# Seven block products in place of eight for 18 couples of an expert layer

## The chip, the core and the metric

The kernel runs on one core of a Trainium2 chip. Five engines work side by side, each on its own list of instructions in order: TensorE (PE) multiplies matrices out of SBUF into PSUM, VectorE (DVE) and ScalarE (ACT) work elementwise and can read PSUM, GpSimd (POOL) works elementwise in SBUF and issues the indirect transfers, SyncE (SP) issues all other transfers. PSUM has 128 partitions in eight banks; one bank holds 128 x 512 numbers of 32 bits. The metric is the time of one execution in microseconds; before the change the median of three runs is 1423.42 us (1422.26 to 1426.2).

## The reference

```python
X = np.fft.rfft(x, axis=1)                       # x: 8 batches of 2496 x 256
Yr = Xr @ w_r - Xi @ w_i + b_r                   # complex mixing, 256 x 256
Yi = Xr @ w_i + Xi @ w_r + b_i
Y  = soft-threshold of Yr and Yi by 0.01
x  = np.fft.irfft(Y, n=2496, axis=1)             # now 19968 tokens of 256
logits = x @ w_gate                              # 8 experts
e_idx  = argmax(logits); gate_w = softmax(logits)[e_idx]
eom    = 1 / (1 + exp(-(x @ w_output_gate)))
for e in range(8):
    h  = np.maximum(x[mask] @ w1[e], 0.0)        # w1[e]: 256 x 1024, the up-product
    ye = h @ w2[e]                               # w2[e]: 1024 x 256, the down-product
    out[mask] = gate_w * eom[:, e] * ye
```

The output is 19968 x 256 in 32-bit floats. The kernel represents a 32-bit number as a high and a low half in 16-bit floats and makes each product of three: high by high, high by low, low by high.

## The kernel before

The first part goes through the eight batches: a Fourier transform in two stages of matmuls (lines 715 and 793), the mixing (823), the inverse in two stages (853 and 919), the gate's logits (964). The tokens with their gate factors are written to a table `yd` in device memory. Meanwhile the expert weights are read, scaled by a power of two for each expert, split into halves (lines 1118 to 1123, on ACT, POOL and DVE) and stored as `wd`, 2 MB for each expert.

Routing runs twice, on DVE above all: `routing(0)` after four batches, `routing(1)` after eight. Each gives tiles of 128 tokens of one expert, with indices to gather their rows and to scatter their results. The 160 tiles are 71 couples of two tiles that share an expert (`PAIRS`, tiles 0 to 141), and 18 mixed tiles of two half tiles of different experts. The first 32 couples (tiles 0 to 63) are of the first phase; couples 32 to 70 are the second phase, with the mixed tiles strewn among them (`BLOCKS`).

For a tile, `gathers` issues the indirect read on POOL; `tokens` finds a scale on DVE (lines 438 to 449), the factor (1507), the high half on ACT (1512) and the low half on DVE (1513), and SP issues a transposing transfer into `eT` (1526). For a couple, `block` starts four pieces of `up`, each filling a PSUM bank with 12 matmuls of 256 token columns (1617): two blocks of 128 hidden units, each 2 halves of the contraction by 3 half products. ACT applies the ReLU and writes the high half of the hidden values (1627), DVE the low half (1628). `down` multiplies by the second weights, one bank a tile with 24 matmuls of 256 columns (1581), ACT scales the result (1597), POOL scatters it (1600).

Weights of couples lie in three buffers `wbuf`, used in turn (`wplace`; the couples of one buffer go through the experts in order, so that most transfers are found unneeded on the chip and skipped). `fetch` and `half_fetch` issue the conditional transfers on SP, the up-half and the down-half of 1 MB each (1461), after the product that last used that half. The mixed tiles have two buffers of their own, laid over the first part's `bt` and `bdt`.

The order of all this isn't found on the chip: `Issue` is a planner that plays the program through while it is built. Each piece of work is a Python generator that yields the engine it needs, a priority (a due time, smaller first) and an assumed duration; when an engine is free in the plan, the waiting piece with the smallest due time is issued. `Slots` and `Places` hold back a piece until a buffer is free, and a bank has to be free for each product. The resulting order of each engine is fixed; on the chip an engine waits for the next instruction of its list. The constants at the head of the file (`P`, `UP`, `DN`, `AHEAD`, `RT`, `WF` and so on) are due times and the depth of lookahead.

```python
i, pt = yield "P", r, 1.42 if len(w) > 1 else (1.34, 1.31)[m - 1], f, True
yield "A", r, 0.6, lambda: A.activation(hv[:, 0], pt, AF.Relu)
yield "D", r, 0.69, lambda: V.scalar_tensor_tensor(hv[:, 1], pt, 0.0, hv[:, 0], ALU.max, ALU.subtract)
```

Of the kernel before, what the change touches and what calls it, by code (L numbers as in the profile page):

```python
# [27 lines left out]
NQ = 22  # L28
P3 = 3 * N1
# [107 lines left out]
P = 69.07  # L137
TP, TE, QT = -14.75, -31.33, 31.33
# [3 lines left out]
S2 = 28.15  # L142
E1 = 55.66
DS = 3.39
ES = 7.69
Z1 = 39.76
Z2 = 21.97
IV = -7.74
IS = 2.63
GO = -33.61  # L150
R0 = 25.15
R1, G1 = 6.43, 0.54
GA = 0.66
W0 = 10.67
W1 = 30.32
TG = 54.25
# [5 lines left out]
XL, TA, TB, YS, WL, WS = -82.07, -9.26, -27.11, 68.34, 21.07, 89.6  # L162
# [3 lines left out]
UP, DN = 1.32, 10.12  # L166
AHEAD = 6
# [3 lines left out]
LR = 9.25  # L171
QN, QY, QV, QX, QZ, QU = -11.85, 13.43, 208.83, 73.36, 34.2, 102.95
RA, QE = -58.63, -33.84
SA = 35.74
SE = 78.16
Z3 = 16.69
BE = 49.35
YE = 51.81
PB = -2.78, -1.54, 0.72, 8.85, 1.32, 0.97, 8.27, 4.18
XC = 7.0, 0.1, 5.4, 0.1, 3.0, 0.1  # L180
RT = -33.27
WT = 0.0
WF = 24.23
QO = -60.23
# [143 lines left out]
def tile_fft_moe(ctx, tc, x, w_r, w_i, b_r, b_i, w_gate, w_og, w1, w2, f1, f4, cmat, gmat, m16, out, dbg=None):  # L328
# [30 lines left out]
    wd = pd.tile([E, 128, 8192], F16, name="wd")  # L359

# [35 lines left out]
    isc = pc.tile([128, E], F32, name="isc")  # L396
    A.activation(isc, cnt[-1], AF.Exp)
# [83 lines left out]
    whl = pf.tile([128, 2, 2, 512], F16, name="whl")  # L481
# [11 lines left out]
    yt = [py.tile([P3, 4, ROW], F32, name=f"yt{i}") for i in range(YR)]  # L493
# [9 lines left out]
    slots = {k: Slots(n) for k, n in dict(x=XR - 6, s1=S1 + 1, A=AN, xt=3, z=2, zhl=ZR, bt=1, bd=1, yt=YR, ol0=OL[0], wr=WR - 1, wsp=SR, ol1=OL[1], fac=12, dg=1, gL=1).items()}  # L503
    slots.update({k: Places(range(EARLY[k])) for k in EARLY})
    slots.update(eT1=Places([]), hh1=Places([]))
# [583 lines left out]
    def weights(r, step):  # L1089

        yield "s1", 0
        for u in range(2 * E):
# [9 lines left out]
            def f():  # L1102
                s, si = root2(ma, "swe")
                if m == 0:
                    V.tensor_copy(isc[:, e:e + 1], si)
                else:
                    V.tensor_tensor(isc[:, e:e + 1], isc[:, e:e + 1], si, ALU.mult)
# [289 lines left out]
    W = []  # L1397
# [12 lines left out]
    def open_h():  # L1410
# [11 lines left out]
        yield "lbm", B - 1  # L1422
        for pool, tag in ((pf, "bt"), (py, "bdt")):
            W.append(pool.tile([128, 4 * NQ * 128], F16, tag=tag, name="late" + tag)[:, :8192])
        late = pf.tile([128, K1 * 256], F16, tag="gt", name="lategt")
        for i in range(2):
            parts_["hh", "late", i] = late[:, 2048 * i:2048 * i + 2048]
            parts_["eT", "late", i] = late[:, 4096 + 512 * i:4608 + 512 * i].rearrange("p (m v c n) -> p m v c n", m=1, v=2, c=2)
            for k in ("hh", "eT"):
                io.put(slots[k + "1"], ("late", i))  # L1430
        io.set("late")
# [5 lines left out]
    def before(k):  # L1437

        return None if k < 2 or k == KW else k - 2 if k < KW else k - 3

    def fetch(r):

        yield "w open"
        for k, (t, n) in enumerate(PAIRS):
# [3 lines left out]
            for m in range(2):  # L1448
# [3 lines left out]
                io.at(io.now + (TAIL if before(k) is None else WT), io.set, "w", t, m, 0)  # L1452

    def half_fetch(key, m, c, place, new, r):
# [8 lines left out]
        yield from move(r, 1.05e6 if new else 0, (1.3, 0.4)[m], f)  # L1463
# [226 lines left out]
```

## Time and profile before

| | us |
|---|---|
| median of three runs | 1423.42 |
| the profiled execution | 1422.78 |
| its span | 1421.0 |
| PE busy | 1390.6 (98%) |
| DVE busy | 986.2 (69%) |
| ACT busy | 738.9 (52%) |
| POOL busy | 650.5 (46%) |
| up-products of couples, line 1617, 3408 matmuls of 256 columns | 389.2 |
| down-products of couples, line 1581, 3408 matmuls of 256 columns | 391.0 |

A row of the groups gives line, engine, operation, output and inputs by their names, the tile's shape, the count, the busy time, the mean of one in ns, and then the idle time of the engine ahead of them. The mean of a matmul holds its way through the array, which overlaps with the next ones; the distance between matmuls is read from the starts in the timeline. PEld are the weight loads, which overlap with the matmuls. A row of the stretches gives busy time and count for each engine, the granted clock of PE as a share of full speed, the share of the transfer engines and GB/s. A row of the waits gives total, times and longest. The timeline has start, duration and instruction; idle time ahead of it stands in brackets.

### The profile page before, as it was taken

The page shows a single profiled execution, that of the slowest core. Times are in us where ns is not written, and L with a number is a line of the kernel's source. Part 1 is how long each engine was busy: PE and PEld are TensorE (multiplying, and loading weights), DVE is VectorE, ACT ScalarE, POOL GpSimd, SP SyncE. Part 2 cuts the span into 40 slices and gives each one's busy share as a digit, 9 for nine tenths or more (in the row PEclk, how much of TensorE's full clock was granted, in tenths as well). Part 3 has the DMA queues.
Part 4 walks back from the last instruction along what each step waited for, and adds up shares of the span by engine and source line. Part 5 has one row for each costly group of instructions (what it writes and reads, how often), then busy time and mean ns, then how long its engine had stood idle before and what let it go on. Part 6 is the DMA issues. An engine that isn't in the chain of part 4 may idle for free.

```text
span 1421.0 us, 40860 instructions
## 1 busy us (share of the span) xinstructions
PE 1390.6 (98%) x15696; PEld 1237.5 (87%) x15696; DVE 986.2 (69%) x2849; ACT 738.9 (52%) x1401; POOL 650.5 (46%) x733
## 2 busy tenths in 40 slices
PE   7999999999999999899999999999999999999996
PEld 5998989898988888789998888999989999999996
DVE  5888877789999888668998774555455545554541
ACT  4877687778677765343333344434444434434431
POOL 3464645564567663334455634343343334333311
PEclk9999999999999999999999999999999999999999
DMA  8699989898988898786353373554644565555440
GB/s 212 166 212 230 205 226 207 214 212 224 217 203 188 201 227 190 196 253 174 97 158 78 88 178 80 135 142 128 164 107 103 135 168 132 135 137 139 126 106 23
DMA packets 285997, 231.54 MB, mean 163 GB/s; under 512 B 239246, under 2 KB 248080, under 8 KB 279167
## 3 DMA queue, kind: packets, MB, share of 16 engines
q1 hardware_dynamic: 270377, 187.02, 54.1%
q0 software_dynamic: 15424, 41.90, 12.7%
q8 instruction: 123, 2.02, 0.6%
q14 instruction: 73, 0.60, 0.1%
HBM read 286.72 MB, written 58.52 MB: 243 GB/s over the span
## 4 chain that ended last, share of the span: by engine, by line
PE 83%; DVE 6%; issue 5%; DMA 2%; POOL 2%; ACT 1%; SPq 1%; POOLq 0%; DVEq 0%; ACTq 0%
PE ps L1617 27%; PE ps L1581 26%; PE ps L823 11%; PE ps L715 5%; PE ps L793 3%; PE ps L919 3%; PE ps L853 3%; DMA x<-in_x 1%; PE ps L964 1%; PE ps L758 1%; POOL out L1600 1%; PE ps L817 1%; PE ps L599 1%; PE ps L1385 1%; DVE z L839 1%
## 5 line engine op out<-in xcount | busy, mean ns | idle before, releaser
L1617 PE MATMUL ps<-eT,wbuf 128*128 128x256 f16 x3408 | 389.2, 273 | 3.6 <-DMA wbuf<-wd 3.6
L1581 PE MATMUL ps<-wbuf,hh 128*128 128x256 f16 x3408 | 391.0, 273 | 0.0
L1617 PEld LDWEIGHTS <-wbuf 128*128 128x128 f16 x3408 | 331.6, 98 | 43.7 <-DMA wbuf<-wd 3.8
L1581 PEld LDWEIGHTS <-hh 128*128 128x128 f16 x3408 | 329.0, 98 | 41.9 <-issue 3.8
L1628 DVE SCALAR_TENSOR_TENSOR hh<-ps,hh 128x512 f16<-128x512 f32 x284 | 196.0, 690 | 225.7 <-ACT hh L1627 224.6
L1600 POOL DMA_INDIRECT out<-o,sidx x160 | 166.0, 1038 | 372.7 <-ACT o L1597 351.6
L1627 ACT ACTIVATE hh<-ps 128x512 f16<-128x512 f32 x284 | 169.5, 597 | 231.7 <-PE ps L1617 229.8
L823 PE MATMUL ps<-whl,xt 128*128 128x256 f16 x1920 | 222.6, 273 | 0.0
L1485 POOL DMA_INDIRECT yg<-yd,gidx x160 | 158.2, 989 | 138.7 <-DVE yhl L1513 82.9
L823 PEld LDWEIGHTS <-xt 128*128 128x128 f16 x1920 | 187.8, 98 | 30.9 <-issue 0.6
L1597 ACT ACTIVATE o<-ps,facs 128x256 f32<-128x256 f32 x160 | 75.7, 473 | 178.5 <-PE ps L1581 169.3
L1512 ACT ACTIVATE yhl<-yg,ys 128x256 f16<-128x256 f32 x160 | 80.8, 506 | 66.9 <-DVE ysi L449 31.7
L715 PE MATMUL ps<-f1t,x 117*128 117x120 f32 (+1 forms) x704 | 90.3, 282 | 9.2 <-DMA x<-in_x 7.8
L715 PEld LDWEIGHTS ps<-f1t,x 117*128 117x128 f32 (+1 forms) x704 | 85.6, 197 | 12.6 <-issue 9.1
L843 POOL TENSOR_TENSOR zhl<-z,zhl 128x512 f16<-128x512 f32 x64 | 75.6, 1182 | 30.8 <-ACT zhl L841 15.4
L1513 DVE SCALAR_TENSOR_TENSOR yhl<-yg,ys,yhl 128x256 f16<-128x256 f32 x160 | 78.9, 509 | 14.1 <-ACT yhl L1512 13.9
L842 POOL CAST zhl<-z 128x512 f16<-128x512 f32 x54 | 34.1, 631 | 107.7 <-DVE z L839 76.6
L838 ACT ACTIVATE zhl<-ps,sc 128x512 f32<-128x512 f32 x80 | 54.8, 686 | 39.1 <-PE ps L823 32.1
L1122 POOL TENSOR_TENSOR wsp<-wr,wsp 128x512 f16<-128x512 f32 x58 | 70.7, 1219 | 4.8
L1628 DVE SCALAR_TENSOR_TENSOR lategt<-ps,lategt 128x512 f16<-128x512 f32 x36 | 24.8, 688 | 65.8 <-ACT lategt L1627 65.8
L839 DVE SCALAR_TENSOR_TENSOR z<-ps,zhl 128x512 f32<-128x512 f32 x80 | 54.6, 684 | 20.7 <-ACT zhl L838 19.4
L919 PE MATMUL ps<-bdt,f4t 120*117 120x512 f16 x264 | 68.8, 379 | 0.0
(236 smaller groups left out, 2113.6 us busy)
## 6 DMA issues: line engine op xcount, KB each, us to landing
wbuf<-wd SPq DMA_DIRECT2D x142, 1024.0 KB
latebt<-wd SPq DMA_DIRECT2D x36, 1024.0 KB
latebdt<-wd SPq DMA_DIRECT2D x36, 1024.0 KB
yd<-yt SPq DMA_DIRECT2D x120, 158.4 KB
x<-in_x SPq DMA_DIRECT2D x106, 156.0 KB
wr<-in_moe_w SPq DMA_DIRECT2D x32, 512.0 KB
wd<-wsp SPq DMA_DIRECT2D x64, 256.0 KB
yg<-yd,gidx POOLq DMA_INDIRECT x160
```

The source lines that it names most:

```text
L715: T.matmul(pv[:, dh, :, m * j:m * j + m], xs[:k, j0 + j, 128 * dh:128 * dh + 128], fw, start=True, stop=True)
L823: T.matmul(yp[:, 256 * j:256 * j + 256], xt_[:, v, 2 * dh + j, 64 - 64 * u:192 - 64 * u], whl[:, dh, vw, 256 * u:256 * u + 256], start=Fal ...
L919: T.matmul(pt[:P3], w, src[:, :, :, vb_], start=(n == 0), stop=(n == 2))
L1485: yield "G", r + 5.6 * POS[t] - 30, 1.0, lambda: G.indirect_dma_start(out=yg, out_offset=None, in_=src, in_offset=bass.IndirectOffsetOnAxi ...
L1512: yield "A", r - 10, 0.5, lambda: A.activation(yhl[:, 0], yg[:, :256], AF.Copy, scale=s)
L1513: yield "D", r - 10, 0.48, lambda: V.scalar_tensor_tensor(yhl[:, 1], yg[:, :256], s, yhl[:, 0], ALU.mult, ALU.subtract)
L1581: T.matmul(st["pt", t][1][c * q:c * q + c, :256], hh[:, v, fc, 128 * n + c * q:128 * n + c * q + c], wq[:, fc // 2, vw, fc % 2], start=(fc ...
L1597: yield "A", r - DN, 0.47, lambda: A.activation(o, pt[:, :256], AF.Copy, scale=fac)
L1600: yield "G", r - DN, 1.0, lambda: G.indirect_dma_start(out=outs[POS[t] % 8], out_offset=bass.IndirectOffsetOnAxis(ap=sidx[:, t:t + 1], axi ...
L1617: T.matmul(pt[:, 128 * m * j:128 * m * (j + 1)][:, 64 * q:128 * m - 64 * (len(w) - 1 - q)], wq[:, dh, g // 4, vw, 128 * (g % 4):128 * (g % ...
L1627: yield "A", r, 0.6, lambda: A.activation(hv[:, 0], pt, AF.Relu)
L1628: yield "D", r, 0.69, lambda: V.scalar_tensor_tensor(hv[:, 1], pt, 0.0, hv[:, 0], ALU.max, ALU.subtract)
```

## The change

For 18 couples of the second phase (tiles from 88 on whose weights are in the first or the second of the three buffers: `seven`) the up-product is made otherwise. Tokens are two blocks of 128 (the two tiles), the contraction two blocks of 128, the hidden units two blocks of 512. The product of two 2 x 2 block matrices takes eight block products; Winograd's form of Strassen's method takes seven, with sums of blocks ahead and behind.

- Sums of weights: four for each expert (S1 to S4 of 256 x 1024 as blocks of 128 x 512). `sums` reads `w1` anew, adds on POOL or DVE, scales and splits on ACT and POOL or DVE, and stores them as `wsd`, 1 MB for each expert. It waits until `routing(1)` is at its end. `sum_fetch` brings them next to the weights, two conditional transfers for each of the couples.
- Sums of tokens: `presum` makes four for each couple on POOL, with ACT for the high half.
- `up7` makes the seven products, each one bank of 4 x 3 matmuls of 128 columns. Their sums: the first bank is copied by ACT, the second added by DVE, the third and fourth copied by ACT and added to on POOL, and four banks are completed by DVE in PSUM, with ReLU on ACT and the low half on DVE as before. Only one couple is within its seven products at a time.
- The low half of odd tiles of these couples is made on POOL in place of DVE.
- `AHEAD` goes from 6 to 10 tiles, the assumed time of a weight transfer from 1.05e6 to 1.4e6 over `RATE`, two assumed durations in `tokens` rise, and nearly all due times have new values, those of the first part too.

```diff
-P = 69.07
+P = 68.59
-UP, DN = 1.32, 10.12
-AHEAD = 6
+UP, DN = 3.46, 8.42
+AHEAD = 10
-RT = -33.27
-WF = 24.23
+F0 = 12
+Q7, F7, S7, D7, Q8 = 52.48, 51.53, 393.97, 9.66, 426.55
+RT = -47.5
+WF = -42.38
...
+    def sums(r):
+
+        yield "late"
+        yield "tiles", 1
+        for e in range(E):
+            yield slots["raw"]
+            raw = st["raw"][e % 2]
+            for i in range(2):
+                yield from move(r + D7 * e, 5.3e5, 0.5, lambda: nc.sync.dma_start(raw[i], w1[e].rearrange("(c p) f -> p c f", p=128)[:, i]))
+            io.go(sums_of(e, raw, r + D7 * e), io.now + TAIL)
+
+    def sums_of(e, raw, r):
+
+        a11, a21, a12, a22 = (raw[i // 2][:, 512 * (i % 2):512 * (i % 2) + 512] for i in range(4))
+        for o, a, b, op in ((a22, a21, a22, ALU.add), (a21, a11, a21, ALU.subtract), (a11, a22, a11, ALU.subtract), (a12, a12, a11, ALU.subtract)):
+            yield either("G", r, 1.25, "D", r + Q7, 1.06, lambda g: g.tensor_tensor(o, a, b, op))
+        s = sws[:, e:e + 1]
+        for i, rv in enumerate((a22, a11, a21, a12)):
+            il = yield slots["t7"]
+            hl = late_tile("zhl", il, [128, 2, 512], F16)
+            yield "A", r, 0.72, lambda: A.activation(hl[:, 0], rv, AF.Copy, scale=s)
+            yield [("G", r, 2.04, multi(
+                       lambda: G.tensor_scalar(rv, rv, s, 1.0, ALU.mult, ALU.mult),
+                       lambda: G.tensor_tensor(hl[:, 1], rv, hl[:, 0], ALU.subtract))),
+                   ("D", r + Q7, 1.12, lambda: V.scalar_tensor_tensor(hl[:, 1], rv, s, hl[:, 0], ALU.mult, ALU.subtract))]
...
+            io.go(sum_out(wsd[e, :, 1024 * i:1024 * i + 1024].rearrange("p (v f) -> p v f", v=2), hl, il, r))
...
+                if m == 0 and seven(t):
+                    yield "sums"
+                    new = not seven(PAIRS[before(k)][0])
+                    yield from sum_fetch(k, wplace(k), new, r + 5.6 * POS[t])
...
-        yield from move(r, 1.05e6 if new else 0, (1.3, 0.4)[m], f)
+        yield from move(r, 1.4e6 if new else 0, (1.3, 0.4)[m], f)
...
+        if seven(t) and t % 2:
+            yield "G", r - 10, 1.2, f
+        else:
+            yield "D", r - 10, 0.53, lambda: V.scalar_tensor_tensor(yhl[:, 1], yg[:, :256], s, yhl[:, 0], ALU.mult, ALU.subtract)
...
+    def seven(t):
+        return T_A + 2 * F0 <= t < T_S and wplace(t // 2) != 2
...
+    def presum(t, eT, r):
...
+        def f(g):
+            g.tensor_tensor(xq[:, 0], xq[:, :, 1], xq[:, 0], ALU.subtract)
+            g.tensor_tensor(xq[:, 1, 1], xq[:, 1, 1], xq[:, 0, 0], ALU.subtract)
+            g.tensor_tensor(xq[:, 1, 0], xq[:, 1, 0], xq[:, 1, 1], ALU.subtract)
+
+        yield "G", r, 1.2, lambda: G.tensor_tensor(xq, e[:, 0], e[:, 1], ALU.add)
+        yield "G", r, 1.75, lambda: f(G)
+        il = yield slots["t7"]
+        th = late_tile("zhl", il, [128, 2, 512], F16)
+        yield "A", r, 0.64, lambda: A.activation(th[:, 0], x, AF.Copy)
+        yield "G", r, 1.2, lambda: G.tensor_tensor(th[:, 1], x, th[:, 0], ALU.subtract)
...
+    def up7(t, w, eT, ie, hh, r):
...
+                for j in range(4):
+                    for n, (va, vx) in enumerate(((0, 0), (0, 1), (1, 0))):
+                        T.matmul(o[:, 128 * j:128 * j + 128], a[:, va, 128 * j:128 * j + 128], x[:, vx], start=(n == 0), stop=(n == 2))
...
+        def second(i, o):
+            yield "7s", t
...
+            yield "D", r, 0.69, lambda: V.tensor_tensor(u["2"], o, u["s"], ALU.add)
...
+        def third(k, i, o, n):
...
+            yield "A", r, 0.6, lambda: A.activation(u[k], o, AF.Copy)
...
+            yield "72", t
+            yield "G", r, 1.3, lambda: G.tensor_tensor(u[k], u[k], u["2"], ALU.add)
...
+        def leave(i, o, k, h, n):
+            yield "7" + k, t
...
+            yield "D", r, 0.69, lambda: V.tensor_tensor(o, o, u[k], ALU.add)
+            used7(k)
+            a = o.rearrange("p (c n) -> p c n", c=4)
+            hq = hh[:, :, 4 * h:4 * h + 4, 128 * n:128 * n + 128]
+            yield "A", r, 0.6, lambda: A.activation(hq[:, 0], a, AF.Relu)
+            yield "D", r, 0.69, lambda: V.scalar_tensor_tensor(hq[:, 1], a, 0.0, hq[:, 0], ALU.max, ALU.subtract)
...
+        i, o = yield "P", r, 0.69, into(w[:, 0, 0], eT[:, 0, :, 0]), True
+        io.go(first(i, o))
+        i, o = yield "P", r + UP, 0.69, into(sv[1], th[:, :, 3]), True
+        io.go(second(i, o))
+        i, o = yield "P", r + UP, 0.69, into(sv[0], th[:, :, 0]), True
+        io.go(third("4", i, o, 2))
+        i, o = yield "P", r + UP, 0.69, into(sv[2], th[:, :, 1]), True
+        io.go(third("3", i, o, 1))
+        io.go(leave(i, o, "4", 1, 1))
+        i, o = yield "P", r + UP, 0.69, into(w[:, 1, 0], eT[:, 0, :, 1]), True
+        io.go(leave(i, o, "s", 0, 0))
+        i, o = yield "P", r + UP, 0.69, into(sv[3], eT[:, 1, :, 1]), True
+        io.go(leave(i, o, "4", 0, 1))
+        i, o = yield "P", r + UP, 0.69, into(w[:, 1, 1], th[:, :, 2]), True
+        io.go(leave(i, o, "3", 1, 0))
```

More of the change, by code (lines that the diff above doesn't have):

```diff
@@ L141 @@
 T1 = 0.91
[L142 to L156, printed above, removed]
+S2 = 15.3
+E1 = 45.23
+DS = 3.5
+ES = 16.61
+Z1 = 17.45
+Z2 = 7.09
+IV = -1.7
+IS = 4.25
+GO = -65.95
+R0 = 31.64
+R1, G1 = 11.89, 0.51
+GA = 0.64
+W0 = 21.97
+W1 = 29.36
+TG = 12.78
 HEAD = 15.0
@@ L492, in tile_fft_moe @@
     at = pm.tile([128, K1, 2, 2, 128], F16, name="at")
-    yt = [py.tile([P3, 4, ROW], F32, name=f"yt{i}") for i in range(YR)]
+    yt = [py.tile([128, 4, ROW], F32, tag=f"yt{i}", name=f"yt{i}")[:P3] for i in range(YR)]
     for y in yt:
@@ L1430, in open_h @@
                 io.put(slots[k + "1"], ("late", i))
+        for k, n in (("z7", 2), ("x7", 3), ("t7", 3)):
+            for i in range(n):
+                io.put(slots[k], i)
         io.set("late")
@@ L1439, in before, with sum_out @@
         return None if k < 2 or k == KW else k - 2 if k < KW else k - 3
+    def sums(r):
[4 more added lines that the diff above has]
+            raw = st["raw"][e % 2]
+            for i in range(2):
+                yield from move(r + D7 * e, 5.3e5, 0.5, lambda: nc.sync.dma_start(raw[i], w1[e].rearrange("(c p) f -> p c f", p=128)[:, i]))
[13 more added lines that the diff above has]
+                   ("D", r + Q7, 1.12, lambda: V.scalar_tensor_tensor(hl[:, 1], rv, s, hl[:, 0], ALU.mult, ALU.subtract))]
+            if i == 3:
+                give("raw")
+            io.go(sum_out(wsd[e, :, 1024 * i:1024 * i + 1024].rearrange("p (v f) -> p v f", v=2), hl, il, r))
+    def sum_out(dst, hl, il, r):
+        yield from move(r, 2.6e5, 0.5, lambda: nc.sync.dma_start(dst, hl))
+        yield TAIL
+        io.put(slots["t7"], il)
+        st["nsum"] = st.get("nsum", 0) + 1
+        if st["nsum"] == 4 * E:
+            io.set("sums")
     def fetch(r):
@@ L1550, in block @@
             yield "w", t, 0, 1
+        if seven(t):
+            io.go(presum(t, eT, r - F7))
+            yield "w", t, 2, 0
+            yield "th", t
+            yield slots["seven"]
         if m == 2:
@@ L1560, in block @@
         st["nu", t] = 0
-        for half in range(2 * m):
+        if seven(t):
+            io.go(up7(t, w[0], eT, ie, hh, r))
+        for half in range(0 if seven(t) else 2 * m):
             io.go(up(t, m, half, w, eT, ie, hh, r + UP * half * (m - 1)))
@@ L1583, in down @@
         for half in range(m):
-            for i in range(2 * half, 2 * half + 2):
-                yield "hh", t0, i
+            if seven(t0):
+                yield "hq", t0, half, n
+            else:
+                for i in range(2 * half, 2 * half + 2):
+                    yield "hh", t0, i
             if half == 0:
```

112 lines of the change are left out of this document (93 added, 19 removed).

## The prediction, made before the result was known

> **What bounds the kernel now.** I read the page's busy times first, then the busy time by stretches, then what TensorE (PE) waited for, and last the single rows that price the edit.
>
> ```profile
> span 1421.0 us, 40860 instructions
> ## 1 busy us (share of the span) xinstructions
> PE 1390.6 (98%) x15696; PEld 1237.5 (87%) x15696; DVE 986.2 (69%) x2849; ACT 738.9 (52%) x1401; POOL 650.5 (46%) x733
> ```
> ```profile
> core 0: us, PE busy (x) PEld busy (x) DVE busy (x) ACT busy (x) POOL busy (x), PEclk, DMA share, GB/s
> 0.00:20.00 20.00, 11.08 (x64) 9.35 (x65) 6.04 (x17) 3.79 (x6) 4.57 (x12) 1.00 0.81 179
> ...
> 20.00:520.00 500.00, 494.53 (x5727) 435.69 (x5726) 431.58 (x1058) 372.83 (x714) 288.48 (x356) 1.00 0.90 210
> ...
> 580.00:600.00 20.00, 16.44 (x130) 13.40 (x129) 11.72 (x50) 5.88 (x12) 6.11 (x8) 0.91 0.71 221
> ...
> 840.00:1040.00 200.00, 200.00 (x2296) 180.25 (x2295) 105.52 (x354) 81.75 (x152) 77.69 (x78) 1.00 0.54 132
> 1049.11:1335.97 286.86, 286.86 (x3552) 259.10 (x3549) 148.04 (x486) 116.56 (x216) 108.59 (x109) 1.00 0.55 134
> ...
> 1400.00:1420.00 20.00, 9.84 (x111) 8.46 (x110) 0.00 (x0) 1.90 (x4) 4.40 (x5) 0.86 0.08 28
> ```
> ```profile
> PE ps L715 <- DMA x<-in_x: 7.8, 1, 7.8
> PE ps L1617 <- DMA wbuf<-wd: 3.6, 1, 3.6
> ```
>
> PE is busy without a gap from 840 on, where the edited couples lie: 200.00 of 200.00 and 286.86 of 286.86 us. There the time is the sum of PE's instructions, and whatever leaves PE there shortens the kernel, as long as no other engine turns late. VectorE (DVE) is busy for 148.04/286.86 = 52% there, ScalarE (ACT) for 41%, GpSimd (POOL) for 38%. PE's idle time lies elsewhere: 8.9 us in the first 20, 5.5 in the next 500, 3.6 at 580 to 600 where a weight load came late, and 10.2 in the last stretch, after its work is done.
>
> **The products.** A couple's up-product is 48 matmuls of 256 columns now; an edited one is seven banks of 4 x 3 = 12 matmuls of 128 columns, 84 in all. Rows of PE's timeline: the two 256-column runs of one couple at full clock, then runs of 128 columns of the earlier stage.
>
> ```profile
> 1352.10 5.40 PE L1617 MATMUL ps<-eT,wbuf 128*128 128x256 f16 x48
> 1357.34 5.40 PE L1581 MATMUL ps<-wbuf,hh 128*128 128x256 f16 x48
> ```
> ```profile
> 343.16 0.83 PE L853 MATMUL ps<-gt,zhl 128*128 128x128 f16 x12
> 343.83 1.46 PE L919 MATMUL ps<-bdt,f4t 120*117 120x512 f16 x6
> 345.12 1.50 PE L793 MATMUL ps<-ct,A 128*128 128x128 f16 x24
> 346.47 0.22 PE L853 MATMUL ps<-gt,zhl 128*128 128x128 f16 x1
> ```
>
> From start to next start, 48 wide matmuls take 1357.34 - 1352.10 = 5.24 us. Twelve narrow ones take 343.83 - 343.16 = 0.67, and 24 take 1.35. Seven banks are then 7 x 0.67 = 4.69 us: not 7/8 of 5.24 (4.585), since every matmul carries a little beside its columns. The gain is 0.55 us a couple, 18 x 0.55 = **9.9 us**.
>
> The Trainium skill ("TensorE: Matmul & The Clock Gate", Back-to-back issue gap) speaks against the change: it says that in a stream of weight loads and matmuls both set the spacing, about 81 ns for 128 columns, and that the formula for one isolated matmul gives too little there. By 81 ns a couple would take 6.80 us, estimated from that page, and the 18 would lose 28 us. The trace disagrees: 1.35 us over 24 matmuls, each with its own load, is 56 ns.
>
> **The work put on the other engines.** Rows of the groups by line:
>
> ```profile
> L843 POOL TENSOR_TENSOR zhl<-z,zhl 128x512 f16<-128x512 f32 x64 | 75.6, 1182 | 30.8 <-ACT zhl L841 15.4 <-DMA A<-at 6.9 <-DMA yd<-yt 4.3
> L1122 POOL TENSOR_TENSOR wsp<-wr,wsp 128x512 f16<-128x512 f32 x58 | 70.7, 1219 | 4.8
> L1121 POOL TENSOR_SCALAR wr<-wr,swe 128x512 f32<-128x512 f32 x58 | 42.2, 728 | 14.9 <-ACT wsp L1118 12.2
> L1377 POOL TENSOR_TENSOR ob<-ob,t 117x256 f16<-117x256 f16 x9 | 5.9, 655 | 5.8 <-DVE gri L1056 1.8 <-DVE p2c L455 1.5 <-DVE ob L1356 1.3
> L654 POOL TENSOR_SCALAR bs<-bias,sc 128x256 f32<-128x256 f32 x8 | 5.1, 641 | 11.7 <-DVE sc L648 11.7
> L1377 POOL TENSOR_TENSOR ob<-ob,t 117x128 f16<-117x128 f16 x2 | 1.1, 546 | 0.8 <-DVE ob L1356 0.8
> ```
> ```profile
> L1628 DVE SCALAR_TENSOR_TENSOR hh<-ps,hh 128x512 f16<-128x512 f32 x284 | 196.0, 690 | 225.7 <-ACT hh L1627 224.6
> L1513 DVE SCALAR_TENSOR_TENSOR yhl<-yg,ys,yhl 128x256 f16<-128x256 f32 x160 | 78.9, 509 | 14.1 <-ACT yhl L1512 13.9
> L839 DVE SCALAR_TENSOR_TENSOR z<-ps,zhl 128x512 f32<-128x512 f32 x80 | 54.6, 684 | 20.7 <-ACT zhl L838 19.4
> L843 DVE TENSOR_TENSOR zhl<-z,zhl 128x512 f16<-128x512 f32 x16 | 15.1, 949 | 0.0
> L1123 DVE SCALAR_TENSOR_TENSOR wsp<-wr,swe,wsp 128x512 f16<-128x512 f32 x6 | 5.9, 975 | 0.0
> ```
> ```profile
> L1627 ACT ACTIVATE hh<-ps 128x512 f16<-128x512 f32 x284 | 169.5, 597 | 231.7 <-PE ps L1617 229.8 <-PE ps L1385 1.7
> L1118 ACT ACTIVATE wsp<-wr,swe 128x512 f16<-128x512 f32 x27 | 19.4, 719 | 1.4 <-DVE swe L460 1.4
> ```
>
> POOL, for each edited couple: two sums of 512 at 1.2 (first sum and low half), 0.655 + 2 x 0.546 = 1.75 for the three differences, two additions of 512 at 1.2, and the odd tile's low half 0.64 + 0.655 = 1.3. That is 4.15 + 2.4 + 1.3 = 7.85 us. An addition with only f32 operands has no row; it lies between one pass (0.73) and two (1.46), and I take 1.2, the nearest two-input rows. DVE: four subtractions out of a bank become one addition and four times an addition and a subtraction, so 9 x 0.69 in place of 4 x 0.69, less 0.51 for the moved low half: 2.94 us more. The addition that writes back into its bank has no row either; 0.684 and 0.949 bound it, the first also reads a bank, so I take 0.69 (with the second, 1.3 us more). ACT: eight passes in place of four, 2.4 us more.
>
> Over some 320 us that hold the 18 couples, by the shares above, POOL goes from 121 to 121 + 141 = 262 of the 310 us left (**85%**), DVE from 165 to 218 (70%), ACT from 130 to 174 (56%). None passes PE, so I cost this work at nothing on the path. Its cover is the order of PE: a couple's down-product comes after the down-product of the couple before. From the end of the first bank the chain is ACT 0.6, DVE 0.69, POOL 1.2, and then four banks each with 1.38 of DVE: about 8.6 us with the hand-overs. PE has six more banks (4.0) and 5.24 of the other down-product to do, 9.2 us. That leaves under a microsecond for the last bank, though the first tile's down-product doesn't need it yet. What is queued behind a late POOL addition is a gather or an output scatter; a bank kept too long holds the next couple's products.
>
> **The sums of weights.** They wait for the end of the second routing, whose last piece is the first row here; the first edited couple's up-product is the second.
>
> ```profile
> 839.10 0.26 DVE L1230 TENSOR_TENSOR isb<-isb,rs 128x96 f32<-128x96 f32 x1
> ```
> ```profile
> 1038.63 5.24 PE ps L1617 x48
> ```
>
> They have 200 us. An expert costs four additions (1.2 on POOL, 0.95 on DVE), four ACT passes of 0.72 and four low halves (0.73 + 1.22 on POOL, 0.975 on DVE). All eight on POOL are 8 x 12.6 = 101 us, and POOL is idle for 200 - 77.69 = 122; on DVE they are 62 of 94.5 idle. Transfers: 1 MB read and 1 MB stored for each expert, 16.8 MB; the window moves 132 GB/s x 200 us = 26.4 MB with a share of 0.54, so 0.34 more, 0.88 together. It fits, at a cost of nothing; the cover is small on POOL and DMA. On SP's queue 16 loads, 32 stores and the new fetches (2 DMAs for each of 18 couples) stand in order with the token transposes; a store waiting for POOL holds the transposes behind it, and PE waits once ten tiles (52 us) of lookahead are used up.
>
> **The other constants** write the order anew, also for the stages that the edit doesn't touch. Their work on PE is the same, so only PE's idle time can change. The late weight load is the largest of it:
>
> ```profile
> 588.95 6.83 PE L1617 MATMUL ps<-eT,wbuf 128*128 128x256 f16 x48 [3.56 <-DMA wbuf<-wd]
> ```
> ```profile
> 583.22 5.68 DMA wbuf<-wd
> ```
>
> It cost 3.56 us of waiting and 6.83 - 5.24 = 1.59 of slow clock, 5.2 in all. The planner's cost of such a load was 1.05e6/225e3 = 4.67 us, under the 5.68 measured; it becomes 6.2, above it, and fetches get an earlier place. The bounds are a gain of 5.2 + 5.5 (all of the idle time between 20 and 520) and a loss of one more stall of this kind, 5.2. I take half of the stall, -2.6, as the load still competes with the transposes there.
>
> **The sum.** The profiled execution took 1422.78 us (span 1421.0 and 1.8 around it), and -9.9 - 2.6 gives 1410.3. The median of the three runs is 0.64 above it: **1411**.
>
> **The rivals.** (a) More: the stall goes whole and half of the 5.5 us too: 1423.4 - 9.9 - 5.2 - 2.8 = 1405.5. For it speaks the new load cost; against it that DVE is at 86% (431.58/500) in the first part. (b) Nothing: the gain is eaten by waits of PE at the first edited couples, where the sums' transfers (0.88 share) hold transposes and fetches back. Two stalls of 5.2 us undo it: 1423.4 - 9.9 + 10.4 = 1424. Against it: at a share of 0.90 the first 500 us lost PE only 5.5. (c) Slower: POOL becomes the bound of the edited couples. It has 320 - 121 = 199 us for its added 141 before the kernel is slower than today, so it decides from 1.41 times my prices; at 1.5 times it needs 121 + 212 = 333, 13 over today's 320, and the couples lose their gain: 1437. For it: the unseen f32 additions, and an in-order queue that also carries gathers and scatters. Against it: 1182 and 1219 ns agree across two lines while DVE was busy. (d) The narrow products are paced by their weight loads, so the change doesn't save PE time: at the 6.80 us above, 1451. The 0.67 us rows speak against it.
>
> **Chances.** Forecast 0.64, (a) 0.10, (b) 0.12, (c) 0.12, (d) 0.02. A change under 0.3% (4.3 us, about what a measurement of this kernel can tell from none) is the middle of (b): same 0.10. Faster is the forecast, (a) and a hundredth of (b): 0.75. Slower is (c), (d) and a hundredth of (b): 0.15. The forecast's own range is 1406 to 1417; with most of (a) and (b) it becomes 1404 to 1424, which leaves out (c), (d) and the end of (a), under 0.2.
>
> **What would show it.** Step one: 1512 matmuls of 128x128 in the new products, at 0.67 us a bank, and 864 fewer of 256 columns in the old line. Step two: PE still without gaps after 1040, POOL at 80 to 88% there, the new additions near 1.2 us. Step three: no PE wait on a fetch of the sums. Step four: the 3.6 us wait gone or smaller. I am wrong if PE shows waits for POOL, for a bank or for a transpose in the edited couples that sum to more than 5 us, or if the first 840 us lose more than one stall.

## The result, and the profile after

The changed kernel takes 1464.58 us (median of four runs, 1453.9 to 1469.73) beside 1424.4 for the kernel before: a ratio of 1.0268, with a 95% interval of 1.0239 to 1.0296. It is slower by some 40 us; 1411 was forecast, and the range ended at 1424. The profiled execution took 1469.73 us, the slowest of the four.

The page of the changed kernel, busy times:

```profile
span 1468.0 us, 42709 instructions
## 1 busy us (share of the span) xinstructions
PE 1399.2 (95%) x16342; PEld 1246.2 (85%) x16342; DVE 1092.7 (74%) x2962; ACT 780.7 (53%) x1491; POOL 849.0 (58%) x948
```

The stretches of the changed kernel (busy time and count by engine, granted clock, share of the transfer engines, GB/s):

```profile
0.00:840.00 840.00, 815.03 (x8719) 717.09 (x8720) 688.66 (x1902) 502.67 (x959) 434.20 (x522) 0.99 0.80 189
840.00:1040.00 200.00, 189.10 (x2058) 167.30 (x2056) 141.88 (x390) 88.99 (x171) 138.42 (x127) 0.97 0.75 200
1040.00:1468.00 428.00, 395.03 (x5571) 361.80 (x5568) 262.19 (x670) 189.05 (x362) 276.36 (x300) 0.97 0.47 129
```

Before, PE had no gap from 840 to 1400. Now it has gaps both where the sums of weights are made (840 to 1040) and where the edited couples run, and the granted clock, 1.00 there before, is 0.97. PE's work should have shrunk to 1390.6 - 9.9 = 1380.7 us; it is busy for 1399.2. So the 47.0 us of added span are -9.9 of work, +18.5 of the same work at a lower clock, and +38.4 of idle time (1468.0 - 1399.2 = 68.8, in place of 30.4). Another profiled execution of the changed kernel, of 1454.67 us, has 30.3 of added idle time and 11.5 of slow work (span 1452.9, PE busy 1392.2).

What PE waited for in the changed kernel (total, times, longest):

```profile
PE ps L1703 <- DMA wbuf<-wd: 6.5, 1, 6.5
PE ps L1703 <- DMA eT<-yhl: 5.5, 2, 5.3
PE ps L1390 <- DVE facs L1576: 5.4, 1, 5.4
PE ps L1664 <- DVE lategt L1714: 4.9, 3, 3.7
PE ps L1664 <- ACT hh L1713: 4.3, 1, 4.3
PE ps L1390 <- POOL ob L1382: 3.8, 3, 2.4
PE ps L1664 <- DVE hh L1813: 3.7, 5, 1.8
PE ps L1664 <- ACT hh L1812: 3.1, 1, 3.1
```

No single cause stands out: a weight load, a transpose, ReLUs on ACT, low halves on DVE, each late once or a few times, by up to 1.8 to 6.5 us. (Line 1703 is the old up-product, 1664 the down-product, 1390 a product of the routing, 1713 and 1714 the ReLU and low half behind the old product, 1812 and 1813 those behind the new one, 1576 the factor, 1760 the new products.) What such a wait costs beyond itself shows in PE's timeline after one of them (start, duration, instruction, the idle time ahead of it in brackets):

```profile
1271.01 2.72 PE L1703 MATMUL ps<-eT,wbuf 128*128 128x256 f16 x12 [5.26 <-DMA eT<-yhl]
1273.52 1.49 PE L1760 MATMUL ps<-eT,wbuf 128*128 128x128 f16 x12
1274.80 2.05 PE L1703 MATMUL ps<-eT,wbuf 128*128 128x256 f16 x12
1276.69 0.83 PE L1760 MATMUL ps<-eT,latewhl 128*128 128x128 f16 x12
1277.36 1.47 PE L1703 MATMUL ps<-eT,wbuf 128*128 128x256 f16 x12
```

Twelve wide matmuls take 1273.52 - 1271.01 = 2.51 us behind the gap (before, 5.24 / 4 = 1.31), and a new bank 1.28. Six microseconds behind the gap a new bank takes 1277.36 - 1276.69 = 0.67, the price of the forecast. The 38.4 us of idle time brought 18.5 us of slow work with them, about half as much on top; in the execution of 1454.67 us it was 11.5 on 30.3, a little over a third. Short gaps don't do it: behind one of 2.38 us (1178.62) six matmuls of 64 columns take 0.34 us as elsewhere, while behind one of 3.07 (1158.07) a run of 22 wide matmuls takes 4.16 us, where 2.58 is usual. The Trainium skill ("TensorE: Matmul & The Clock Gate", What's actually happening) says that PE's clock falls to half after an idle window of about 3.4 us and comes back after about as long a busy one; the halved speed behind this 5.26-us gap agrees, and so does its end, 3.8 to 5.7 us behind the gap (between 1274.80 and 1276.69), if a little late.

### The profile page after: what moved, and what is told of

It is laid out like the page before. It is cut to its first block, busy times and chain, and to the rows that moved or that the text cites. A ratio compares the mean times of both kernels' runs of the same rounds, so it can differ in the third digit from the quotient of the medians.

```text
span 1468.0 us, 42709 instructions
## 1 busy us (share of the span) xinstructions
PE 1399.2 (95%) x16342; PEld 1246.2 (85%) x16342; DVE 1092.7 (74%) x2962; ACT 780.7 (53%) x1491; POOL 849.0 (58%) x948
## 5 line engine op out<-in xcount | busy, mean ns | idle before, releaser
L1664 PE MATMUL ps<-wbuf,hh 128*128 128x256 f16 x3408 | 401.7, 274 | 11.8 <-ACT hh L1713 4.3
L1703 PE MATMUL ps<-eT,wbuf 128*128 128x256 f16 x2544 | 304.1, 277 | 12.0 <-DMA wbuf<-wd 6.5
L1703 PEld LDWEIGHTS <-wbuf 128*128 128x128 f16 x2544 | 250.0, 99 | 46.0 <-DMA wbuf<-wd 6.7
L1554 POOL DMA_INDIRECT yg<-yd,gidx x160 | 161.3, 1008 | 103.5 <-issue 32.1
L1714 DVE SCALAR_TENSOR_TENSOR hh<-ps,hh 128x512 f16<-128x512 f32 x212 | 144.4, 686 | 71.3 <-ACT hh L1713 70.1
L1589 DVE SCALAR_TENSOR_TENSOR yhl<-yg,ys,yhl 128x256 f16<-128x256 f32 x142 | 89.2, 633 | 36.2 <-ACT yhl L1581 36.2
L847 POOL TENSOR_TENSOR zhl<-z,zhl 128x512 f16<-128x512 f32 x68 | 79.9, 1177 | 23.2 <-ACT zhl L845 13.2
L442 DVE TENSOR_REDUCE yms<-yg 128x1 f32<-128x256 f32 x160 | 64.1, 409 | 18.2 <-DMA yg<-yd,gidx 18.2
L843 DVE SCALAR_TENSOR_TENSOR z<-ps,zhl 128x512 f32<-128x512 f32 x80 | 54.6, 682 | 18.8 <-ACT zhl L842 18.4
```

Of the source, the lines that this page charges most:

```text
L847: yield either("G", r - Z3, 1.2, "D", r - Z3 + QY, 1.0, lambda e: e.tensor_tensor(zhl[:, 1], z, zhl[:, 0], ALU.subtract))
L1554: yield "G", r + 5.6 * POS[t] - 30, 1.0, lambda: G.indirect_dma_start(out=yg, out_offset=None, in_=src, in_offset=bass.IndirectOffsetOnAxi ...
L1589: yield "D", r - 10, 0.53, lambda: V.scalar_tensor_tensor(yhl[:, 1], yg[:, :256], s, yhl[:, 0], ALU.mult, ALU.subtract)
L1664: T.matmul(st["pt", t][1][c * q:c * q + c, :256], hh[:, v, fc, 128 * n + c * q:128 * n + c * q + c], wq[:, fc // 2, vw, fc % 2], start=(fc ...
L1703: T.matmul(pt[:, 128 * m * j:128 * m * (j + 1)][:, 64 * q:128 * m - 64 * (len(w) - 1 - q)], wq[:, dh, g // 4, vw, 128 * (g % 4):128 * (g % ...
```

## The experiments

Four theories stood at first. **A**: the new due times and the deeper lookahead cost the time. **B**: the sums of weights do, because ACT and DVE, each with its fixed list, stand behind their transfers. **C**: DVE is held up by POOL's many tensor operations. **D**: the new couples do, because POOL is held longer by an indirect transfer than its busy time says. Two came later. **F**: transfers bunch where the expert changes. **G**: weight loads stand behind transposes in SP's queue.

Runs were made in five comparisons; ratios are to the kernel before in the same one. In the first and the fourth (before: 1455.8 and 1456.21 us, in place of about 1425) the traces show PE idle for 3 to 17 us with no releaser, and at most 0.9 us elsewhere. Why is open, and not every kernel loses the same there: the kernel before lost some 32 us, the one with the due times alone 4 (1431.33 beside 1427.34). So times and ratios from these two prove little, and their traces have to carry the argument. The unchanged kernel, run again, gave 1.0004 (0.9993 to 1.0016) in the second and 0.9993 (0.9982 to 1.0003) in the fifth.

**The due times alone.** No couple is edited and no sums are made; all constants are the new ones.

```diff
-        return T_A + 2 * F0 <= t < T_S and wplace(t // 2) != 2
+        return False
-    io.go(sums(P * B + RT + S7))
```

> The changed kernel with no couple edited: the test that picks the 18 couples is never true and the sums of weights are not made. What is left of the change are the due times, the lookahead and the assumed durations. Theory A (the new due times make the order of the untouched stages worse): the first 840 us lose some 12 us more than before, as in the changed kernel, and the time is about 1436. Theory B (the sums' transfers land late and hold ACT and DVE) and theory C (DVE instructions with two inputs in SBUF are blocked by the added POOL instructions) both expect the time of before or a little less, 1418 to 1426, and PE without waits after 840.

It took 1431.33 us in the first comparison (0.9827, beside a kernel before of 1455.8). Made again in the third:

> The kernel with the due times alone once more, beside a before that should be near 1425, since its first run fell on a chip where before took 1456. Theory A: 1431 to 1436, 6 us or more over before. If the due times are innocent: 1420 to 1427.

1427.34 us, 1.0016 (1.0001 to 1.0031): at most a few microseconds slower, 1424 x 0.0016 = 2.3. PE runs from 840 to 1400 without a gap. A falls.

**The old due times with the edit.** The values of before for all but the new constants.

```diff
-UP, DN = 3.46, 8.42
-AHEAD = 10
+UP, DN = 1.32, 10.12
+AHEAD = 6
...
```

> The changed kernel with the due times and the lookahead of before; only the constants that the new pieces need keep their new values. Theory A: the 12 us of the first 840 us come back, about 1452, and if the thin order of the edited couples is also a matter of the due times, about 1425. Theories B and C: no gain, 1460 to 1470, since the same sums and the same POOL instructions are there.

1498.33 us, 1.0278 (1.0232 to 1.0323); two smaller edits of the changed kernel, below, took 1475.48 and 1476.14 beside it. PE waits 8.9 us for transposes of couples and 10.3 for those of mixed tiles, where the changed kernel waits 5.5 and 2.4. So with the edit the old due times do worse, not better.

**The assumed landing of the sums' transfers.** `TAIL`, 1.7 us, becomes 9.0 behind the loads and stores of `sums`.

```diff
-            io.go(sums_of(e, raw, r + D7 * e), io.now + TAIL)
+            io.go(sums_of(e, raw, r + D7 * e), io.now + 9.0)
...
-        yield TAIL
+        yield 9.0
```

> The changed kernel in which the plan assumes 9 us in place of 1.7 until a load or a store of the sums has landed; the measured landings were near 8. Theory B: ACT and DVE no longer stand before a transfer in the stretch of the sums, the two stalls near 957 and 1005 (idle 4.3 + 0.7 + 1.2 + 3.7 and the slow clock behind them, about 16 us) go, about 1449. Theories A and C: the same time within 5 us, 1460 to 1470.

1475.48 us, 1.0135 (1.0101 to 1.017). The stalls between 950 and 1005 are gone, but the sums now end after the first edited couple needs them. PE's waits in this kernel:

```profile
PE ps L1760 <- DMA latebt<-wsd: 9.9, 1, 9.9
```

No operation of ACT or DVE in the sums waits for a load or a store any more. The mechanism of B is shown, and that a long assumption for all of these transfers moves its cost instead of ending it.

**DVE without its second operand.** The factor of a tile is one value for each partition; its form with two full operands is replaced by one with two scalars.

```diff
-            V.scalar_tensor_tensor(fac, yg[:, 256:257], si, route["is"][:, t:t + 1], ALU.mult, ALU.mult)
+            V.tensor_scalar(fac, yg[:, 256:257], si, route["is"][:, t:t + 1], ALU.mult, ALU.mult)
```

> The changed kernel with the order of every engine kept; only the factor of a token tile is made by a tensor_scalar with two pointer scalars in place of an instruction with two inputs in SBUF. Theory C: this instruction takes about 0.2 us everywhere in place of 0.47 in the mean after 840, DVE gets 24 us back there, and the waits of PE for DVE in the edited couples shrink: 1450 to 1458. Theories A and B: its duration doesn't matter, 1460 to 1470.

1476.14 us, 1.0141 (1.0106 to 1.0176). The group of this operation from 840 on, in the kernel before, the changed one, and this one:

```profile
L1507 DVE SCALAR_TENSOR_TENSOR facs<-yg,ysi,isb 128x1 f32<-128x1 f32 x103 | 22.7, 220 | 3.6
```
```profile
L1576 DVE SCALAR_TENSOR_TENSOR facs<-yg,ysi,isb 128x1 f32<-128x1 f32 x101 | 46.1, 457 | 3.5
```
```profile
L1576 DVE TENSOR_SCALAR facs<-yg,ysi,isb 128x1 f32<-128x1 f32 x98 | 26.8, 273 | 3.6
```

DVE does lose time to POOL, 46.1 - 22.7 = 23.4 us on this operation alone, and gets most of it back here. But PE still stalls near 953, 1001, 1157, 1178, 1273 and 1345, the places where the changed kernel does. C is real and doesn't decide.

**Products alone and sums alone.** In the second comparison the change was taken apart, with the changed kernel beside it.

> The changed kernel, unchanged, with a profile on the same chip: 1455 to 1480. The base for the next two and for the runs on single parts; its loss against before is to be split by the next two runs and the run with the due times alone.

1458.34 us, 1.0239 (1.0215 to 1.0263). Its stretches:

```profile
840.00:1040.00 200.00, 189.87 (x2062) 168.18 (x2060) 138.22 (x380) 90.07 (x173) 144.39 (x131) 0.97 0.76 205
1040.00:1400.00 360.00, 340.30 (x4892) 312.29 (x4890) 240.28 (x627) 167.37 (x321) 249.57 (x272) 0.98 0.52 139
```

Products alone: the sums aren't made, and the fetches bring as many bytes of the plain weights.

```diff
-                    yield "sums"
-                nc.sync.dma_start(a, wsd[ds(f, 1), ...
+                nc.sync.dma_start(a, wd[ds(f, 1), ...
-    io.go(sums(P * B + RT + S7))
```

> The changed kernel with the seven products but without making the sums of weights: nothing is read, added or stored for them, and the fetch of the sums reads the same number of bytes from the stored weights instead, so the edited couples compute with other numbers. Theory B (the sums' transfers hold ACT and DVE): the stalls at 940 to 1010 go, 16 us or more, about 1445. Theory C (the added POOL and DVE work of the edited couples makes chains late): the stalls between 1120 and 1360 stay, some 30 us against before, and the time stays above 1445. Theory A: the first 840 us lose the same 12 us as with the due times alone.

1446.63 us, 1.0146 (1.0118 to 1.0175):

```profile
840.00:1040.00 200.00, 200.00 (x2288) 180.25 (x2287) 120.92 (x382) 80.44 (x153) 83.27 (x89) 1.00 0.56 141
1040.00:1400.00 360.00, 340.11 (x4838) 312.41 (x4835) 234.48 (x615) 165.08 (x318) 248.36 (x271) 0.97 0.50 136
```

Sums alone: they are made and fetched, and the couples keep their eight products (an `edited(t)` that is always False takes the place of `seven(t)` where products and token sums are chosen).

> The changed kernel with the sums of weights made, stored and fetched, but with eight products for every couple and the low halves on DVE as before: the 9.9 us on PE are not saved. Theory B: the stalls at 940 to 1010 stay (16 us) and nothing else beyond the due times alone, so about 16 us over that run, 1447. Theory C: about the run with the due times alone, 1431 to 1436, with PE without waits after 1040.

1439.5 us, 1.0098 (1.0066 to 1.013):

```profile
840.00:1040.00 200.00, 188.67 (x2062) 167.66 (x2060) 140.64 (x380) 89.16 (x172) 139.25 (x127) 0.97 0.76 205
1040.00:1400.00 360.00, 360.00 (x4500) 325.25 (x4499) 188.08 (x576) 139.51 (x268) 124.48 (x126) 1.00 0.54 144
```

The parts come apart by place. From 840 to 1400 the sums cost PE time only up to 1040, and the products only behind it. Sums alone cost 1439.5 - 1425.55 = 14.0 us, products alone 21.1, both with the 2.3 of the due times; 14.0 + 21.1 - 2.3 = 32.8, and the whole costs 1458.34 - 1425.55 = 32.8. That it fits to the tenth is chance: the 2.3 comes from another comparison, and the changed kernel's own runs spread over 7.6 us here. But nothing large is left for the two together.

How the sums do it shows in the changed kernel. Its chain of waits (start, us, what):

```profile
945.32 7.70 DMA wsd<-zhl
```

ACT's timeline there:

```profile
953.02 0.72 ACT L1478 ACTIVATE zhl<-latebdt,sws 128x512 f16<-128x512 f32 x1 [9.80 <-DMA wsd<-zhl]
...
956.07 0.58 ACT L1713 ACTIVATE hh<-ps 128x512 f16<-128x512 f32 x1
```

and PE's:

```profile
956.70 0.61 PE L1664 MATMUL ps<-wbuf,hh 128*128 128x256 f16 x2 [4.29 <-ACT hh L1713]
```

A store of sums takes 7.70 us to land. The plan has 1.16 us for it on SP's queue (2.6e5 / 225e3) and 1.7 behind that, 2.9 in all. The next sum's pass over ACT needs that buffer. In ACT's list it stands ahead of a ReLU of an unedited couple, so ACT stands still for 9.80 us, and PE runs out of hidden values. DVE stands the same way for 7.45 us ahead of 993.19, there for a load of raw weights.

**The same order with lighter work.** In the third comparison the order is that of the changed kernel. First POOL's operations work on a few columns only:

```diff
-G.tensor_tensor(u[k], u[k], u["2"], ALU.add)
+G.tensor_tensor(u[k][:, :32], u[k][:, :32], u["2"][:, :32], ALU.add)
...
```

> The changed kernel, order of every engine kept, with some 3.8 us less POOL work for each edited couple: the three differences, the two additions behind the products and the scaling of the odd tile go over a few columns only, so the edited couples' numbers are wrong. Theory D (POOL, whose indirect transfers take 1.03 us and 0.15 to 0.30 more before the next starts where the plan has 1.0, falls behind in the edited couples, and gathers and sums of products come late): the stalls of the first half of the edited couples (0.8, 3.3, 0.7, 2.3 us idle and the slow clock behind them) go, 10 us or more, about 1446 where before is 1425. Theory F (the late waits are transfers: at a change of expert three loads of 1 MB go ahead of the tokens' transposes): those waits stay, 4 and 7 us, and at most 3 us are won. The sums' stalls (some 17 us) stay by both.

1452.44 us, 1.0185 (1.0164 to 1.0207): (1.0239 - 1.0185) x 1425 = 7.7 us less than the changed kernel, by the ratios of two comparisons. The waits for DVE and ACT that the changed kernel has at 1120 and 1146 in the second comparison are gone but for 0.2 us, those for transfers stay:

```profile
PE ps L1703 <- DMA wbuf<-wd: 6.9, 1, 6.9
PE ps L1703 <- DMA eT<-yhl: 4.7, 2, 4.3
PE ps L1703 <- DMA lategt<-yhl: 3.5, 1, 3.5
```

Then the sums are brought whole where an edited couple is the first in its buffer, and in 64 columns after that:

```diff
+                w = 1024 * n if new else 64
```

> The changed kernel, order kept, in which the fetch of the sums at a change of expert brings 64 columns of each piece in place of all (the first fetch of each buffer stays whole), so the edited couples compute with partly old sums. Theory F: the wait for a transpose (3.9 to 5.3 us) and the wait for a weight load (6.5 to 7 us) near the end go or halve, with the slow clock some 10 us, about 1448. Theory D: they stay, within 3 us of the changed kernel, 1455 to 1461.

1457.63 us, 1.0235 (1.0218 to 1.0252): the wait for the transpose falls to 2.7 us and the one for the weights to 4.6, and the time hardly moves. The 1448 of theory F isn't met. Both together, with the lighter factor of DVE, in the fourth comparison:

> The changed kernel, order of every engine kept, with three lightenings at once: the POOL work over a few columns, the fetch of the sums at a change of expert cut to 64 columns, the factor of a tile made with one input in SBUF. The edited couples' numbers are wrong. If theory D and theory F together are the loss in the edited couples, PE waits less than 4 us after 1040 and the time is about 1440 (the sums' stalls of 17 us stay, the 9.9 us are won). If waits of 4 us or more for a transpose or a weight load stay, the rest comes from where SP's queue has these transfers (theory G: a load stands behind transposes that wait for DVE), and the time is 1447 or more.

1469.41 us, 1.0117 (1.0062 to 1.0171). Transfers are still late, by 2.0 to 3.9 us, 9.9 in all, where the changed kernel of the second comparison has 13.2 (7.0, 3.9 and 2.3). So the amount of work of POOL, of DVE's factor and of the fetches explains only a part of those waits. Another part is their place. SP's queue in the changed kernel, in the second comparison, ahead of the longest wait:

```profile
1313.30 4.64 SPq L1602 DMA_TRANSPOSE eT<-yhl  x2
1318.30 3.43 SPq L1530 DMA_DIRECT2D wbuf<-wd  x3
```

The weight load leaves behind two transposes that had themselves waited for DVE (theory G). Its landing, in the chain of waits of the same kernel:

```profile
1319.89 7.77 DMA wbuf<-wd
...
1327.70 2.31 PE ps L1703 x10
```

The other place is a change of expert, where weights and sums are really brought and a transpose stands behind them (theory F). The plan knows nothing of it: except for the first load of each buffer it counts a conditional fetch as skipped, with 0 bytes and no time until it has landed (`1.4e6 if new else 0`, `WT = 0.0`). In SP's queue a skipped one takes 0.07 us and a real one 0.34 or more. Of SP's queue there, in the same kernel:

```profile
1245.61 0.36 SPq L1530 DMA_DIRECT2D wbuf<-wd  x1
...
1248.16 0.37 SPq L1519 DMA_DIRECT2D latebt<-wsd  x1
1248.83 0.34 SPq L1519 DMA_DIRECT2D latewhl<-wsd  x1
1249.27 1.22 SPq L1602 DMA_TRANSPOSE eT<-yhl  x1
```

The last transpose lands 7.43 us after 1249.27, where the plan has 1.2 on the queue and 1.7 behind it.

**What an indirect transfer takes of POOL.** The trace of before already showed it, in POOL's timeline:

```profile
1063.40 1.01 POOL L1600 DMA_INDIRECT out<-o,sidx  x1 [0.30 <-ACT o L1597]
1064.72 0.97 POOL L1485 DMA_INDIRECT yg<-yd,gidx  x1 [0.30 <-issue]
1065.99 1.01 POOL L1600 DMA_INDIRECT out<-o,sidx  x1 [0.30 <-issue]
```

They follow one another at 1.27 to 1.32 us, 0.30 of it idle with nothing that POOL waits for; the plan has 1.0. With 1.32 in the plan for gathers and scatters:

```diff
-yield "G", r - DN, 1.0, lambda: G.indirect_dma_start(
+yield "G", r - DN, 1.32, lambda: G.indirect_dma_start(
...
```

> The changed kernel, correct numbers, in which the plan takes 1.32 us for a gather or scatter in place of 1.0. The order changes. Theory D: the plan no longer runs ahead of POOL, the edited couples lose 10 us less, about 1448. Theory F and theory B: the waits for transfers stay and the time is 1455 to 1465. If the order alone (any new order with these due times) moves the stalls about, the time may go either way by 10 us.

1443.35 us, 1.0144 (1.0122 to 1.0167). By the ratios of two comparisons that is (1.0239 - 1.0144) x 1425 = 13.5 us less than the changed kernel, from two numbers of the plan. The order is a new one too, so not all of this need be POOL's doing; but it is more than the 10 us allowed above for any new order. D is likely a part of the cause, and only a part: transfers are still late (one wait of 6.0 us), and so is DVE in the sums (3.1).

**All assumed durations nearer to the measured.** Products alone, with 1.32 and with 4.0 in place of 1.7 behind a transpose:

> The seven products without the making of the sums (other bytes of the stored weights in their place, so the edited couples' numbers are wrong), and a plan that takes 1.32 us for a gather or scatter and 4.0 in place of 1.7 until a transpose of the second phase has landed. Theories D and G: with the plan near the measured times the products give their 9.9 us, or most: 1415 to 1424, below before. If the products cost more than PE's rows say (a chain too long for any order), the time stays at 1435 to 1447.

1443.49 us, 0.9917 (0.99 to 0.9933), in the fourth comparison; apart from idle time without a releaser one long wait of 6.2 us is left. Then the whole change with both, with 7.0 for the landing of the sums' transfers, DVE's lighter factor and two couples fewer:

```diff
-F0 = 12
+F0 = 15
...
-        yield TAIL
+        yield 4.0 if t >= T_A else TAIL
```

> A whole and correct kernel: 16 edited couples in place of 18 (the first two left as they were, so the sums have 26 us more), and a plan with 1.32 us for a gather or scatter, 7.0 until a load or store of the sums has landed, 4.0 until a transpose has; the factor of a tile with one input in SBUF. Theories B, D and G together: no stall at the sums, few in the couples, 16 x 0.55 = 8.8 us won against the due times alone: 1418 to 1428. If a transfer-bound rest remains: 1430 to 1443.

1439.44 us, 0.9893 (0.9876 to 0.9909). As a ratio to a kernel that was disturbed itself this proves little, so it was run again in the fifth comparison:

> The correct kernel with 16 edited couples and the longer times in the plan once more, beside a before near 1424. Its trace lost some 6 us to one late transpose and little else after 840. Theories B, D and G: 1420 to 1428. If the edited couples still cost more than they save against the due times alone (1427): 1430 to 1440.

**1419.48 us** (1416.89 to 1421.25) beside 1425.42: 0.9958 (0.9943 to 0.9974), a gain of 5.9 us over the kernel before. That is at the lower end of the 1420 to 1428 expected by theories B, D and G. Its stretches:

```profile
840.00:1040.00 200.00, 200.00 (x2296) 180.26 (x2295) 149.71 (x410) 99.41 (x185) 134.78 (x128) 1.00 0.84 215
1040.00:1400.00 360.00, 356.08 (x5092) 328.57 (x5089) 233.21 (x612) 172.54 (x326) 246.16 (x268) 1.00 0.53 139
```

and the one wait of PE above 1 us in total between 840 and 1400:

```profile
PE ps L1703 <- DMA eT<-yhl: 3.4, 2, 2.3
```

POOL is busy for 246.16 us from 1040 to 1400, about as long as in the changed kernel (249.57), and PE hardly waits. What differs is when each thing was expected, the form of DVE's factor (which alone left the stalls in place) and the two couples.

Last, 7.0 behind the transposes in place of 4.0, for theory F:

> The same with 7.0 in place of 4.0 assumed until a transpose of the second phase has landed. The late transpose took 6.3 us behind two loads of 1 MB at a change of expert. Theory F: this last stall goes, some 5 us less than the run beside it, 1416 to 1424, at or below before. If the order alone decides where stalls fall: within 10 us of the run beside it, either way.

1419.6 us, 0.9964 (0.9951 to 0.9977): the same, with one wait of 3.8 us for a transpose left. F's cure brings nothing. It also bears on a last rival, that any new order moves the stalls about by chance: here two different orders with the longer durations come out alike.

## Why the prediction was wrong

**Step one, the products: right.** The new line has 1512 matmuls of 128 columns and the old one 864 fewer. A bank takes 0.67 us at full clock. The whole kernel bears it out where PE seldom waits: the 16 couples of the repaired version should leave 1390.6 - 16 x 0.55 = 1381.8 us of PE's work, and 1383.1 were measured. Rival (d), products paced by their weight loads, falls: 0.67 / 12 is 56 ns, not 81.

**Step two, the work on the other engines: the step that failed most.** "None passes PE, so I cost this work at nothing on the path." The prices were good. POOL's groups of the changed kernel:

```profile
L1800 POOL TENSOR_TENSOR xt<-xt,z 128x512 f32<-128x512 f32 x36 | 45.8, 1284 | 15.0 <-ACT xt L1795 13.1 <-DVE p2c L447 1.6
L1744 POOL TENSOR_TENSOR zhl<-xt,zhl 128x512 f16<-128x512 f32 x18 | 21.3, 1181 | 3.3 <-ACT zhl L1743 3.2
L1739 POOL TENSOR_TENSOR xt<-eT 128x512 f32<-128x512 f16 x18 | 21.0, 1167 | 16.6 <-DMA eT<-yhl 16.4
L1735 POOL TENSOR_TENSOR xt<-xt 128x256 f32<-128x256 f32 x18 | 13.4, 744 | 0.9
```

With the differences of 128 columns (463 and 459 ns) and the odd tile's low half (508 and 675) a couple costs POOL 2 x 1.284 + 1.181 + 1.167 + 0.744 + 0.922 + 1.183 = 7.77 us, where 7.85 was forecast. The share, too, was below the forecast: 249.57 / 360 = 69% in the second comparison. What failed is the inference from shares. I had worked out "under a microsecond" of cover for the last bank and asked only whether an engine's total fits. In lists fixed beforehand, a piece that is late by a few microseconds holds all that stands behind it, whatever the engine's share, and the plan behind these lists was too hopeful by 0.3 us for each gather and scatter, by several us for transposes, and took the weight loads of a change of expert at nothing. Products alone lose 21.1 - 2.3 = 18.8 us against the due times alone. With the gain of 9.9 in it, that leaves some 28.7 us of waits and slow clock. POOL's 0.30 us behind each indirect transfer stood in the trace that I quoted from, but a sum of busy times doesn't hold it.

**Step three, the sums: failed.** "It fits, at a cost of nothing". They cost 14.0 - 2.3 = 11.7 us. The shares stayed below the forecast (POOL busy for 138.42 of 200 us where I had 77.69 + 101, DMA at 0.75 where I had 0.88); again time was lost by lateness. I saw that a store waiting for POOL would hold transposes on SP; what came was ACT and DVE standing still for 9.80 and 7.45 us until a store and a load had landed.

**Step four, the other constants: wrong in sign, small.** The weight stall at 583 is gone (PE has 20.00 of 20.00 us from 580 to 600; the load now starts at 577.89). My reason for it was not right: beside its 4.67 us the plan has 1.7 until the load has landed, 6.37 in all, so it wasn't under the 5.68 measured. But other stalls came, the longest the 5.4 us of line 1390 in the routing (it isn't there in the execution of 1454.67 us), and the due times by themselves cost 2.3 us, where I had a gain of 2.6.

**The rivals.** (b) named the right mechanism in the wrong place: the sums' transfers stall PE, yet through ACT and DVE in the unedited couples, not through fetches at the first edited ones; that its two stalls of 5.2 us, 10.4, are near the 11.7 measured is luck. (c) named the right place, the edited couples, with the wrong mechanism: POOL wasn't full, it and others were late. Each was priced alone; both together would have been 1437 + 10.4 = 1447, still outside the range and under the 1464.58.

**Open.** How the gain from 1458 to 1419 us divides among the parts of the repaired version wasn't tried, except for the 13.5 us that came with the indirect transfers. Why lighter work in the same order left transposes and weight loads late is only partly explained by SP's queue and by loads that the plan doesn't count; neither was tested by itself. Why the kernel before took 1456 us in two comparisons isn't known.

## What to carry to other kernels

Where the order of each engine is fixed beforehand, a share of busy time below 100% doesn't make added work free: look up the assumed duration of each added piece and of its neighbours in the plan, compare it with the trace, start to start and issue to landing, and count what stands behind it in the same list. An edit that takes 10 us off the bound engine needs each new wait to be shorter than its cover, and the waits here cost a third to a half on top through the clock. Before such an edit is given up, correct the plan's durations: here that, with two couples fewer and another form of DVE's factor, turned 2.4% slower into 0.4% faster.

## What was not expected of the hardware

- **An indirect transfer** holds POOL for about 1.3 us: 1.0 busy and 0.30 before the next one can begin. Behind a tensor operation the gap is mostly 0.14 to 0.17.
- **Landings under load.** A 256 KB store took 7.70 us, the weights in `wbuf` 7.77, a transposing transfer 7.43 behind real loads, where the plan has 2.9 us in all for a transpose or a store. PE's stalls went with late landings, not with the transfer share: from 840 to 1040 and from 1040 to 1400 it was 0.76 and 0.52 in the changed kernel, 0.84 and 0.53 in the repaired version.
- **Tiny operations of DVE beside a busy POOL.** The factor, one value for each partition, went from 220 to 457 ns on average. From 840 to 1400 in the changed kernel, 53 of 98 overlap no tensor operation of POOL and take 243 ns on average; 32 begin while one runs and take 532, up to 1190; 13 have one begin in their time and take 1197, up to 1900. The long ones end when POOL's operation does, as here at 1168.37 and 1168.35:

```profile
1166.47 1.90 DVE L1576 SCALAR_TENSOR_TENSOR facs<-yg,ysi,isb 128x1 f32<-128x1 f32 x1
```
```profile
1167.18 1.17 POOL L1744 TENSOR_TENSOR zhl<-xt,zhl 128x512 f16<-128x512 f32 x1
```

  In the form with scalars each takes 270 to 280 ns in the same stretch, whatever POOL does. The Trainium skill ("SBUF — State Buffer", Who interferes with whom) says that a DVE instruction with two SBUF inputs contends with a GpSimd instruction that reads SBUF, and one with at most one input doesn't, outside its 2-port modes. Both forms agree with it here: 243 ns against 532 and 1197 for the form with two inputs, and no difference for the form with scalars.
- **Idle time of PE with no releaser**, mostly in pieces of 0.3 to 1.2 us and 3 to 17 us in all, in every trace of two comparisons and at most 0.9 in the rest. One piece of 5.34 us, at 953 in the kernel with DVE's other factor, lies where the changed kernel waits for ACT and is likely that wait. The cause of the others was not found.
